# Moving low-part subtractions from GpSimd to VectorE, a scaling from VectorE to ScalarE, and repacing a weight conversion

## The chip, the cores and the metric

The kernel runs on one core of one Trainium2 chip. The metric is device time in microseconds (us) of one execution, and the median of several runs is quoted. The engines of a core each work through their own queue in program order: TensorE (PE in the rows; PEld is its weight load), VectorE (DVE), ScalarE (ACT), GpSimd (POOL) and SyncE (SP), which issues the DMAs.

## The reference

An attention layer over 2 batches, 8 heads, 576 positions and head width 64, with a position bias from a small network, gives 1152 rows of 512 values. Two gated layers follow, the second behind an RMS norm:

```python
def _moe_ref(x, w_gate, w_val, w_out):            # first layer
    gate = 1.0 / (1.0 + np.exp(-(x @ w_gate)))
    val = x @ w_val
    return (gate * val @ w_out).astype(np.float32)
...
    # second layer
    rms = np.sqrt(np.mean(x * x, axis=-1, keepdims=True) + 1e-06)
    xn = x / rms * rms_g
    g = xn @ w_gate
    silu = g * (1.0 / (1.0 + np.exp(-g)))
    val = xn @ w_val
    return (silu * val @ w_out).astype(np.float32)
```

`w_gate` and `w_val` are 512x1536, `w_out` is 1536x512. The weights arrive as 64-bit floating-point words.

## The kernel before, in words

Every product of the gated layers is made of three matmuls on rounded operands: a value is split in a high part (a copy to the type fp32r, on ScalarE) and a low part (the value less its high part). Names ending in `h` are high parts (`wh`, `xh`, `gh`, `nh`), names ending in `l` are low parts (`wl`, `xl`, `gl`, `nl`).

**Steps.** After the attention, the gated layers run as 72 steps `s`, a Python loop at L718 that writes out the order of all instructions by hand. A step is one block of 128 hidden columns (`f`) for one chunk of 384 rows (`c`). `STEPS` orders them by layer, group of blocks (`GROUPS`: 2, 3, 3, 4 blocks in the first layer, 4, 4, 4 in the second), chunk and block. In step `s` the program first calls `gate_val(s)`: 24 matmuls in two PSUM banks (L479), the gate on ScalarE (`sg`, L483), the product with it on VectorE (`g32`, shown as `g`, L485), its high part on ScalarE (`gh`, L487) and its low part (`gl`, L489). Then, between two halves of conversion work, it calls `out_mm(s - 2)`: 12 matmuls (L505) that add into two double banks `acc`. The PSUM pool `ps1` has four banks, so that `gate_val(s)` waits for the banks of step `s - 2`, which `sg` and `g` have to have read. A step whose successor has another group or chunk is called closing: after its `out_mm` the four banks are collected into `part` (L513, L515, L517), and the next `out_mm` can start only then. With blocks of 2, 3, 3, 4 and then 4 the closing `out_mm` falls in steps 3, 5, 7, 10, 13, and so on to 25, and then in every fourth step from 29 to 69.

**Norm.** When a chunk of the first layer is complete (in steps 29, 33 and 37), `norm_stage` runs in stages: squares on ScalarE and two adds on GpSimd (`nrm`, L544 to L546); two steps later a matmul that sums them (`ss`, L551) and a reciprocal root in small VectorE instructions (L555 to L567); one step later a matmul that spreads it (`rb` of L571), the scaling, and the split in `nh` (L577) and `nl` (L578). Step 36 is the first that reads `nh` and `nl`.

**Conversion.** The 72 weight pieces (128x512 each) are loaded as raw words (`wr`, three buffers) and converted. `piece_step(k, i)` has four parts, which this document calls by what they write: part 0 is `tt` (VectorE); part 1 is `ab` as an absolute value (ScalarE, L450), `ff` (VectorE, L452), `rb` (the low words scaled, L454) and the integer add of the two (GpSimd, L455); part 2 is the product `ab` (VectorE, L459) and `wh` (ScalarE, L460); part 3 is `wl` (VectorE, L464). `advance(limit, micro)` writes out up to `micro` parts that are ready, going round through the parts with the counter `phase`. In each half of a step the loop asks for 4 parts when the next piece is needed within 6 steps (`slack < 6`), else for 2. In the step where a closing `out_mm` falls the first half gets none. A piece is four parts.

Of the kernel before, what the change touches and what calls it, by code (L numbers as in the profile page):

```python
# [8 lines left out]
F32 = mybir.dt.float32  # L9
F32R = mybir.dt.float32r  # L10
U32 = mybir.dt.uint32
I32 = mybir.dt.int32
AF = mybir.ActivationFunctionType
ALU = mybir.AluOpType
# [7 lines left out]
NCC = DM // 128  # L22
NF = DFF // 128
CH = 384
# [44 lines left out]
def fused_kernel(ctx: ExitStack, tc: tile.TileContext, qk, vp, tab, pcol, invp, prm, wts, rg, out):  # L69
    nc = tc.nc  # L70
# [8 lines left out]
    def bank(nm):  # L79
        return ps1.tile([128, 512], F32, tag="one", name=nm)  # L80
# [335 lines left out]
    gt = {}  # L416
# [20 lines left out]
    def piece_step(k, i):  # L437
        mc = pools["mc"]
        if i == 0:
            tt = mc.tile([128, 512], U32, tag="tt", name=f"tt{k}")  # L440
            nc.vector.tensor_scalar(  # L441
                tt, wraw[k][:, :, 1], 3, 0x3FFFFFFF, op0=ALU.logical_shift_left, op1=ALU.bitwise_and
            )
            mid[k] = tt
        elif i == 1:
            raw = wraw.pop(k)
            lw, hw = raw[:, :, 0], raw[:, :, 1]
            tt = mid[k]
            ab = mc.tile([128, 512], F32, tag="ab", name=f"ab{k}", bufs=3)
            nc.scalar.activation(ab, hw.bitcast(F32), AF.Abs)  # L450
            ff = mc.tile([128, 512], U32, tag="ff", name=f"ff{k}", bufs=2)
            nc.vector.scalar_tensor_tensor(ff, hw, 0xC0000000, tt, op0=ALU.bitwise_and, op1=ALU.bitwise_or)  # L452
            rb = mc.tile([128, 512], I32, tag="rb", name=f"rb{k}")
            nc.vector.tensor_scalar(rb, lw, 2.0**-29, None, op0=ALU.mult)  # L454
            nc.gpsimd.tensor_tensor(ff.bitcast(I32), ff.bitcast(I32), rb, op=ALU.add)  # L455
            mid[k] = (ab, ff)
        elif i == 2:
            ab, ff = mid[k]
            nc.vector.scalar_tensor_tensor(ab, ab, TINY_HI, ff.bitcast(F32), op0=ALU.is_ge, op1=ALU.mult)  # L459
            nc.scalar.activation(ring[k % RING][0], ab, AF.Copy)  # L460
        else:
            ab, _ = mid.pop(k)
            hi, lo = ring[k % RING]
            nc.vector.tensor_tensor(lo, ab, hi.bitcast(F32), op=ALU.subtract)  # L464
            wp[PIECES[k]] = (hi, lo)

    def gate_val(s):
        l, g, c, f = STEPS[s]
        xhi, xlo = xs[l, c]
        mc = pools["mc"]  # L470
        pss = []
        for w in range(2):
            hi, lo = wp[l, f, w]
            ps = bank(f"gv{s}_{w}")
            k = 0
            for cc in range(NCC):
                cs = slice(cc * 128, cc * 128 + 128)
                for wt, xt in ((hi, xhi), (hi, xlo), (lo, xhi)):
                    nc.tensor.matmul(ps[:, :CH], wt[:, cs], xt[:, cc, :], start=(k == 0), stop=(k == 11))  # L479
                    k += 1  # L480
            pss.append(ps)
        sg = mc.tile([128, CH], F32, tag="sg", name=f"sg{s}")
        nc.scalar.activation(sg, pss[0][:, :CH], AF.Sigmoid if l == 0 else AF.Silu)  # L483
        g32 = mc.tile([128, CH], F32, tag="g32", name=f"g32_{s}", bufs=2)
        nc.vector.tensor_tensor(g32, pss[1][:, :CH], sg, op=ALU.mult)  # L485
        gh = mc.tile([128, CH], F32R, tag="gh", name=f"gh{s}", bufs=3)
        nc.scalar.activation(gh, g32, AF.Copy)  # L487
        gl = mc.tile([128, CH], F32R, tag="gl", name=f"gl{s}", bufs=3)
        nc.gpsimd.tensor_tensor(gl, g32, gh.bitcast(F32), op=ALU.subtract)  # L489
        gt[s] = (gh, gl)  # L490

    def out_mm(s):
# [44 lines left out]
    def norm_stage(c, stage, box):  # L537
        mc = pools["mc"]
        cs = slice(c * CH, c * CH + CH)
        sq = nrm[0][:, : NCC * CH].rearrange("p (a c) -> p a c", a=NCC)  # L540
        dg = nrm[0][:, NCC * CH : NCC * CH + 384].rearrange("p (a c) -> p a c", a=3)
        if stage == 0:
            for m in range(NCC):
                nc.scalar.activation(sq[:, m], part[m][:, cs], AF.Square)  # L544
            nc.gpsimd.tensor_tensor(sq[:, 0:2], sq[:, 0:2], sq[:, 2:4], op=ALU.add)
            nc.gpsimd.tensor_tensor(sq[:, 0], sq[:, 0], sq[:, 1], op=ALU.add)  # L546
            return
        if stage == 1:
            ssp = bank(f"ss{c}")
            for m in range(3):  # L550
                nc.tensor.matmul(  # L551
                    ssp[:, m : m + 1], sq[:, 0, m * 128 : m * 128 + 128], ones[:, 0:1], start=True, stop=True
                )
            ve = mc.tile([128, 3], F32, tag="ve", name=f"ve{c}")
            nc.vector.tensor_scalar(ve, ssp[:, 0:3], 1.0 / DM, 1e-6, op0=ALU.mult, op1=ALU.add)  # L555

            r0 = mc.tile([128, 3], F32, tag="r0", name=f"r0{c}")
            t1 = mc.tile([128, 3], F32, tag="t1", name=f"t1{c}")
            half = t1.bitcast(I32)
            nc.vector.tensor_scalar(half, ve.bitcast(I32), 1, None, op0=ALU.logical_shift_right)  # L560
            nc.vector.tensor_scalar(r0.bitcast(I32), half, -1.0, float(0x5F3759DF), op0=ALU.mult, op1=ALU.add)
            for _ in range(3):
                nc.vector.scalar_tensor_tensor(t1, r0, -0.5, r0, op0=ALU.mult, op1=ALU.mult)
                nc.vector.tensor_tensor(t1, t1, ve, op=ALU.mult)
                nc.vector.scalar_tensor_tensor(r0, t1, 1.5, r0, op0=ALU.add, op1=ALU.mult)
            for m in range(3):
                nc.vector.tensor_scalar(dg[:, m], ident, r0[:, m : m + 1], None, op0=ALU.mult)  # L567
            return
        rbp = bank(f"rb{c}")
        for m in range(3):  # L570
            nc.tensor.matmul(rbp[:, m * 128 : m * 128 + 128], ones, dg[:, m], start=True, stop=True)  # L571
        nh = xp.tile([128, NCC, CH], F32R, tag="xh", name=f"nh{c}")
        nl = xp.tile([128, NCC, CH], F32R, tag="xl", name=f"nl{c}")
        for m in range(NCC):
            x = part[m][:, cs]
            nc.vector.scalar_tensor_tensor(x, x, rgs[:, m : m + 1], rbp[:, :CH], op0=ALU.mult, op1=ALU.mult)
            nc.scalar.activation(nh[:, m], x, AF.Copy)  # L577
            nc.gpsimd.tensor_tensor(nl[:, m], x, nh[:, m].bitcast(F32), op=ALU.subtract)  # L578
        xs[1, c] = (nh, nl)

    done = [0, 0, 0, 0]
# [6 lines left out]
    def deadline(k):  # L588
        return USES[PIECES[k][:2]][0]

    def closing(s):
        return 0 <= s < NS - 1 and STEPS[s][:3] != STEPS[s + 1][:3]

    def ready(i):
        k = done[i]
# [12 lines left out]
    def advance(limit, micro):  # L608
        room[0] = limit
        idle = 0  # L610
        while micro and idle < 4:
            while loaded[0] < NPC and done[1] >= loaded[0] - 2:
                piece_load(loaded[0])
                loaded[0] += 1
            i = 3 - phase[0]
            phase[0] = (phase[0] + 1) % 4
            if ready(i):
                piece_step(done[i], i)
                done[i] += 1
                micro -= 1  # L620
                idle = 0
            else:
                idle += 1
# [94 lines left out]
    for s in range(NS + 2):  # L718
        while s < NS and (STEPS[s][0], STEPS[s][3], 1) not in wp:
            advance(done[3] + 1, 1)  # L720
        if 0 < s < NS:
            gate_val(s)
        for half in range(2):
            k = done[3]
            if k < NPC:
                lim = k
                while lim < NPC and lim < k + 3 and (lim < RING or released(lim - RING) <= s):
                    lim += 1
                slack = deadline(k) - s
                micro = 4 if slack < 6 else 2  # L730

                if closing(s - 2):
                    micro = (0, micro) [half] if slack > 1 else micro
                advance(lim, micro)
            if half == 0:
                if s > 1:
                    l, _, _, f = STEPS[s - 2]
                    while (l, f, 2) not in wp:
                        advance(done[3] + 1, 1)
                    out_mm(s - 2)  # L740
                while norm_queue and norm_queue[0][0] <= s:
                    _, c, stage, box = norm_queue.pop(0)
                    norm_stage(c, stage, box)
                    if stage < 2:
                        norm_queue.append([s + 2 - stage, c, stage + 1, box])


# [66 lines left out]
```

## Time and profile before

| what | value |
|---|---|
| median of 3 runs | 671.61 us (669.06 to 672.57) |
| the profiled execution's own time | 668.84 us |
| its span in the profile | 667.1 us |
| TensorE busy | 644.4 us, 97% of the span |
| VectorE busy | 494.6 us, 74% |
| ScalarE busy | 315.0 us, 47% |
| GpSimd busy | 316.6 us, 47% |

The span is what the profiler recorded between the first and the last instruction; 1.7 us of the execution's own time lie outside it. Busy shares are means over stages of very different kinds, and a matmul counts as busy until its modelled end, so consecutive matmuls overlap in the rows.

### The profile page before, as it was taken

To read this page: it belongs to the slowest core of one execution; us is meant where nothing else is said; L and a number is where in the kernel's file an instruction comes from. 1 tells how busy PE (TensorE), PEld (TensorE's weight loads), DVE (VectorE), ACT (ScalarE), POOL (GpSimd) and SP (SyncE) were. 2 spreads that over 40 slices of the span, in tenths; PEclk is the share of its full clock that TensorE was granted. 3 is DMA by queue.
4 is the path that set the end of the run, shared out by engine and by line. 5 is a ranking of instruction groups with operands and counts; after the bars stand their busy time and mean duration, and the time that the engine had idled before them with its cause. 6 is when DMAs were issued, how large, how long until landed. Compare 5 with 4: busy or idle time off the path is not lost.

```text
span 667.1 us, 11785 instructions
## 1 busy us (share of the span) xinstructions
PE 644.4 (97%) x4354; PEld 573.8 (86%) x4354; DVE 494.6 (74%) x965; ACT 315.0 (47%) x671; POOL 316.6 (47%) x319
## 2 busy tenths in 40 slices
PE   9799999999999799999999999889999999999997
PEld 5245557776689799999999999889999999999997
DVE  7699985788889986887799679989959658621211
ACT  6357778998784443333343345353544323311110
POOL 2246555887675443453444456565735434311111
PEclk9899999999999999999999999989999999999999
DMA  6879768998523342231233311322214322000111
GB/s 186 251 260 306 239 192 260 298 279 279 175 90 110 118 127 64 94 126 65 83 108 103 98 56 62 116 74 64 85 73 127 95 63 64 1 1 0 49 49 47
DMA packets 31642, 82.35 MB, mean 123 GB/s; under 512 B 3552, under 2 KB 5216, under 8 KB 31584
## 3 DMA queue, kind: packets, MB, share of 16 engines
q1 hardware_dynamic: 30720, 80.42, 38.3%
q10 hardware_dynamic: 864, 1.18, 0.5%
q8 instruction: 34, 0.56, 0.3%
q14 instruction: 24, 0.20, 0.1%
HBM read 68.33 MB, written 13.25 MB: 122 GB/s over the span
## 4 chain that ended last, share of the span: by engine, by line
PE 77%; DVE 12%; DMA 5%; issue 3%; ACT 1%; POOL 1%; SPq 1%; DVEq 0%; ACTq 0%; POOLq 0%
PE gv L479 40%; PE pv L369 4%; PE tp L349 4%; PE bps L190 4%; PE s L272 3%; DMA bias_d<-be 2%; DMA bt<-bias_d 2%; DVE ab L459 2%; DVE ff L452 2%; DVE t L290 1%; PE s L266 1%; DVE ht L176 1%; DVE tt L441 1%; DVE rb L454 1%; DVE wv L464 1%
## 5 line engine op out<-in xcount | busy, mean ns | idle before, releaser
L489 POOL TENSOR_TENSOR gl<-g,gh 128x384 fp32r<-128x384 f32 x72 | 85.9, 1192 | 165.0 <-ACT gh L487 165.0
L455 POOL TENSOR_TENSOR ff<-ff,rb 128x512 int32<-128x512 int32 x72 | 95.1, 1321 | 98.8 <-DVE rb L454 96.1
L485 DVE TENSOR_TENSOR g<-gv,sg 128x384 f32<-128x384 f32 x72 | 40.0, 555 | 114.1 <-PE gv L479 102.1
L487 ACT ACTIVATE gh<-g 128x384 fp32r<-128x384 f32 x72 | 37.9, 526 | 132.9 <-DVE g L485 131.5
L479 PE MATMUL gv<-xh,wh 128*128 128x384 f32 x240 | 81.1, 338 | 0.0
L479 PE MATMUL gv<-xh,wl 128*128 128x384 f32 x240 | 80.8, 336 | 0.0
L479 PE MATMUL gv<-xl,wh 128*128 128x384 f32 x240 | 80.7, 336 | 0.0
L460 ACT ACTIVATE wh<-ab 128x512 fp32r<-128x512 f32 x54 | 34.2, 633 | 76.2 <-DVE ab L459 75.7
L323 POOL TENSOR_SCALAR p<-p,rs 128x576 f32<-128x576 f32 x72 | 62.3, 876 | 15.9 <-DVE rs L321 13.0
L459 DVE SCALAR_TENSOR_TENSOR ab<-ab,ff 128x512 f32<-128x512 f32 x72 | 67.2, 933 | 1.2 <-POOL ff L455 1.2
L479 PE MATMUL gv<-nh,wh 128*128 128x384 f32 x192 | 65.4, 341 | 0.0
L479 PE MATMUL gv<-nl,wh 128*128 128x384 f32 x192 | 65.0, 338 | 0.0
L479 PE MATMUL gv<-nh,wl 128*128 128x384 f32 x192 | 64.9, 338 | 0.0
L483 ACT ACTIVATE sg<-gv 128x384 f32<-128x384 f32 x72 | 34.8, 484 | 59.2 <-PE gv L479 58.9
L290 DVE CUSTOM_DVE_ANT_0 t<-s,bt 128x576 f32<-128x576 f32 x72 | 51.7, 751 | 14.0 <-DMA bt<-bias_d 5.7
L176 DVE TENSOR_SCALAR ht<-w1l,bpc 128x448 f32<-128x448 f32 (+17 forms) x131 | 60.6, 527 | 2.1 <-PE bps L190 1.9
L464 DVE TENSOR_TENSOR wl<-ab,wh 128x512 fp32r<-128x512 f32 x54 | 62.1, 1149 | 0.0
L311 ACT ACTIVATE p<-t,mn 128x576 f32<-128x576 f32 x72 | 55.2, 768 | 8.8 <-DVE mn L290 8.6
L452 DVE SCALAR_TENSOR_TENSOR ff<-wr,tt 128x512 uint32<-128x512 uint32 x72 | 56.7, 787 | 0.0
L190 PE MATMUL bps<-ht,prms 128*32 128x264 f32 (+17 forms) x352 | 44.1, 493 | 5.5 <-DVE ht L176 4.4
L369 PEld LDWEIGHTS pv<-pt,v 128*64 128x64 f32 (+1 forms) x640 | 34.3, 136 | 16.3 <-ACT pt L656 4.0
L369 PE MATMUL pv<-pt,v 128*64 128x128 f32 (+3 forms) x640 | 48.1, 293 | 0.0
(455 smaller groups left out, 1588.1 us busy)
## 6 DMA issues: line engine op xcount, KB each, us to landing
wr<-wts SPq DMA_DIRECT2D x72, 512.0 KB, 3.6
bt<-bias_d SPq DMA_DIRECT2D x32, 576.0 KB, 5.1
bias_d<-be SPq DMA_DIRECT2D x36, 295.5 KB, 3.2
raw<-qk SPq DMA_DIRECT2D x16, 288.0 KB, 5.6
v<-vp SPq DMA_DIRECT2D x8, 480.0 KB, 6.3
bt<-bias_d SPq DMA_DIRECT2D x16, 144.0 KB, 5.2
out<-part SPq DMA_DIRECT2D x6, 192.0 KB, 1.9
out<-part ACTq DMA_DIRECT2D x6, 192.0 KB, 1.9
```

The lines of the kernel that those rows point to most:

```text
L176: nc.vector.tensor_scalar(ht, src, bpc[:, t : t + 1], 0.0, op0=ALU.add, op1=ALU.max)
L190: nc.tensor.matmul(ps[cg * 32 : cg * 32 + 32, :cut], prms[:, 2:34], hs[cg][:, a : a + cut], start=True, stop=True)
L290: nc.vector.tensor_tensor_reduce(t, sp[:, :, :288], bt[:, j].rearrange("p (a c) -> p a c", a=2), -SCALE, 3.0e38, ALU.add, ALU.min, mn[:, j ...
L311: nc.scalar.activation(p[:, j], t.rearrange("p a c -> p (a c)"), AF.Exp, bias=mn[:, j : j + 1], scale=-1.0, accum_out=sm[:, j : j + 1],)
L323: nc.gpsimd.tensor_scalar(p[:, j], p[:, j], rs[:, j : j + 1], 1.0, op0=ALU.mult, op1=ALU.mult)
L369: nc.tensor.matmul(box["ps"][j * 64 : j * 64 + 64, :n], v[:k, 2 * j if it == 4 else j, c, :], pt[:k, c, j * 64 : j * 64 + 64] if it == 4 e ...
L452: nc.vector.scalar_tensor_tensor(ff, hw, 0xC0000000, tt, op0=ALU.bitwise_and, op1=ALU.bitwise_or)
L455: nc.gpsimd.tensor_tensor(ff.bitcast(I32), ff.bitcast(I32), rb, op=ALU.add)
L459: nc.vector.scalar_tensor_tensor(ab, ab, TINY_HI, ff.bitcast(F32), op0=ALU.is_ge, op1=ALU.mult)
L464: nc.vector.tensor_tensor(lo, ab, hi.bitcast(F32), op=ALU.subtract)
L479: nc.tensor.matmul(ps[:, :CH], wt[:, cs], xt[:, cc, :], start=(k == 0), stop=(k == 11))
L489: nc.gpsimd.tensor_tensor(gl, g32, gh.bitcast(F32), op=ALU.subtract)
```

## The change

The low parts `gl` and `nl` and the two adds of the norm go from GpSimd to VectorE. The scaling `rb` goes from VectorE to ScalarE. `gl` is written out by a function of its own, after the first half of the step's conversion. The norm's adds get a stage of their own, one step after the squares, so that the two later stages fall in the same steps as before. The counter `phase` starts at another part. A new function `pace(s)` decides the number of parts of a whole step: 2 while a stage of the norm is due, 8 when the next piece is needed within 6 steps, else 4, split over the halves, or all of them in the second half where a closing `out_mm` falls.

```diff
-            nc.vector.tensor_scalar(rb, lw, 2.0**-29, None, op0=ALU.mult)
+            nc.scalar.activation(rb, lw, AF.Copy, scale=2.0**-29)
...
-        gl = mc.tile([128, CH], F32R, tag="gl", name=f"gl{s}", bufs=3)
-        nc.gpsimd.tensor_tensor(gl, g32, gh.bitcast(F32), op=ALU.subtract)
+        gt[s] = (gh, g32)
+
+    def low_part(s):
+        gh, g32 = gt[s]
+        gl = pools["mc"].tile([128, CH], F32R, tag="gl", name=f"gl{s}", bufs=3)
+        nc.vector.tensor_tensor(gl, g32, gh.bitcast(F32), op=ALU.subtract)
         gt[s] = (gh, gl)
...
-            nc.gpsimd.tensor_tensor(sq[:, 0:2], sq[:, 0:2], sq[:, 2:4], op=ALU.add)
-            nc.gpsimd.tensor_tensor(sq[:, 0], sq[:, 0], sq[:, 1], op=ALU.add)
             return
         if stage == 1:
+            nc.vector.tensor_tensor(sq[:, 0:2], sq[:, 0:2], sq[:, 2:4], op=ALU.add)
+            nc.vector.tensor_tensor(sq[:, 0], sq[:, 0], sq[:, 1], op=ALU.add)
+            return
+        if stage == 2:
...
-            nc.gpsimd.tensor_tensor(nl[:, m], x, nh[:, m].bitcast(F32), op=ALU.subtract)
+        for m in range(NCC):
+            x = part[m][:, cs]
+            nc.vector.tensor_tensor(nl[:, m], x, nh[:, m].bitcast(F32), op=ALU.subtract)
...
+    def pace(s):
+        if any(q[0] <= s for q in norm_queue):
+            return 2
+        return 8 if done[3] < NPC and deadline(done[3]) - s < 6 else 4
...
-            i = 3 - phase[0]
+            i = (2, 1, 0, 3)[phase[0]]
...
+        micro = pace(s)
+
+        parts = (0, micro) if closing(s - 2) else (micro // 2, micro - micro // 2)
         for half in range(2):
             k = done[3]
             if k < NPC:
...
-                slack = deadline(k) - s
-                micro = 4 if slack < 6 else 2
-
-                if closing(s - 2):
-                    micro = (0, micro) [half] if slack > 1 else micro
-                advance(lim, micro)
+                advance(lim, parts[half])
             if half == 0:
+                if s < NS:
+                    low_part(s)
                 if s > 1:
...
-                    if stage < 2:
-                        norm_queue.append([s + 2 - stage, c, stage + 1, box])
+                    if stage < 3:
+                        norm_queue.append([s + 1, c, stage + 1, box])
```

## Rows read from the trace of the kernel before

**Rows 1.** Busy time by stretch: start:end, length, each engine's busy us, clock, DMA.

```profile
120.00:190.00 70.00, 67.38 (x687) 50.28 (x684) 58.28 (x158) 60.65 (x158) 54.25 (x68) 1.00 0.78 241
190.00:245.00 55.00, 50.74 (x307) 48.03 (x306) 49.31 (x75) 27.59 (x54) 29.97 (x25) 1.00 0.36 114
392.00:440.00 48.00, 43.76 (x252) 43.44 (x251) 43.07 (x81) 19.69 (x36) 25.73 (x20) 0.96 0.25 84
440.00:653.00 213.00, 213.00 (x1229) 212.50 (x1228) 126.13 (x201) 69.22 (x132) 82.52 (x67) 1.00 0.18 56
```

**Rows 2.** Waits of TensorE from 125 us on: total us, times, longest.

```profile
PE rb L571 <- DVE nrm L567: 4.2, 1, 4.2
PE acc001a L505 <- ACT part L517: 3.4, 1, 3.4
PE s L266 <- DVE mn L290: 1.3, 5, 0.4
PE tp L349 <- DVE pt L654: 1.3, 3, 0.7
PE acc002a L505 <- ACT part L517: 0.9, 1, 0.9
```

**Rows 3.** Chain that ended last, 385 to 470 us: start, us, what.

```profile
405.17 0.67 PE rb L571 x6
...
431.48 1.67 DVE wv L464
...
435.76 1.65 PE rb L571 x6
437.41 4.98 PE gv L479 x24
...
444.46 4.18 PE gv L479 x24
```

**Rows 4.** Timeline of VectorE: start, us, engine, line, operation, idle before in brackets.

```profile
232.92 0.42 DVE L441 TENSOR_SCALAR tt<-wr 128x512 uint32<-128x512 uint32 x1
233.26 1.78 DVE L464 TENSOR_TENSOR wl<-ab,wh 128x512 fp32r<-128x512 f32 x1
234.96 0.68 DVE L459 SCALAR_TENSOR_TENSOR ab<-ab,ff 128x512 f32<-128x512 f32 x1
235.56 0.68 DVE L452 SCALAR_TENSOR_TENSOR ff<-wr,tt 128x512 uint32<-128x512 uint32 x1
236.16 0.41 DVE L454 TENSOR_SCALAR rb<-wr 128x512 int32<-128x512 uint32 x1
...
237.28 0.56 DVE L485 TENSOR_TENSOR g<-gv,sg 128x384 f32<-128x384 f32 x1 [0.70 <-ACT sg L483]
...
279.04 0.56 DVE L485 TENSOR_TENSOR g<-gv,sg 128x384 f32<-128x384 f32 x1 [0.70 <-ACT sg L483]
...
287.32 0.56 DVE L485 TENSOR_TENSOR g<-gv,sg 128x384 f32<-128x384 f32 x1 [0.71 <-ACT sg L483]
...
414.31 2.35 DVE L452 SCALAR_TENSOR_TENSOR ff<-wr,tt 128x512 uint32<-128x512 uint32 x1
```

**Rows 5.** Timeline of ScalarE in the same stretch as Rows 4.

```profile
235.67 0.63 ACT L460 ACTIVATE wh<-ab 128x512 fp32r<-128x512 f32 x1 [2.38 <-DVE ab L459]
236.21 0.66 ACT L450 ACTIVATE ab<-wr 128x512 f32<-128x512 f32 x1
236.77 0.48 ACT L483 ACTIVATE sg<-gv 128x384 f32<-128x384 f32 x1
237.93 0.53 ACT L487 ACTIVATE gh<-g 128x384 fp32r<-128x384 f32 x1 [0.68 <-DVE g L485]
```

**Rows 6.** Timeline of GpSimd, the same stretch, and the norm's first add.

```profile
233.14 1.34 POOL L455 TENSOR_TENSOR ff<-ff,rb 128x512 int32<-128x512 int32 x1 [1.63 <-DVE rb L454]
236.72 1.29 POOL L455 TENSOR_TENSOR ff<-ff,rb 128x512 int32<-128x512 int32 x1 [2.24 <-DVE rb L454]
238.53 1.00 POOL L489 TENSOR_TENSOR gl<-g,gh 128x384 fp32r<-128x384 f32 x1 [0.52 <-ACT gh L487]
...
414.26 1.85 POOL L545 TENSOR_TENSOR nrm<-nrm 128x768 f32<-128x768 f32 x1 [0.41 <-ACT nrm L544]
```

## The prediction

> **What bounds the kernel now.** I read the busy time by stretch first [rows 1]. TensorE is busy in 213.0 of 213 us after 440 us and has holes in three stretches: 2.6 us in the attention (120 to 190), 4.3 us at the start of the gated layers (190 to 245) and 4.2 us around the first layer's end (392 to 440). VectorE is no bound on average, but it is busy for 43.1 of 48 us in the last of them. Then the waits of TensorE say who ended each hole [rows 2]: 3.4 and 0.9 us before the first out_mm of the second and third chunk (acc001a, acc002a), which wait for the collects; 4.2 us before rb of L571, in the norm; and 2.6 us in eight short waits for VectorE in the attention. The chain shows that the hole of 4.2 us costs more than itself [rows 3]: after it the six matmuls of rb take 1.65 us, not 0.67, and the next gate_val 4.98, not 4.18. That is 1.8 us at the lower of the two granted clocks (1.2 of 2.4 GHz); over the stretch of 48 us it makes the mean 0.96 [rows 1]. So about 10 us can be won in all, and anything that makes VectorE or ScalarE late at a closing step can be lost.
>
> The timelines show why VectorE is late [rows 4, 6]. Its instructions with SBUF operands alone do not run beside GpSimd's: wl at 233.26 took 1.78 us, because the add of 233.14 ran until 234.48; the next ab took 0.68. ff at 414.31 took 2.35 us behind the norm's first add, which ended at 416.11.
>
> **The change part by part.** Start to start, [rows 4 to 6] give VectorE 0.34 us for tt and for rb, 0.60 for ff, ab and wl, 0.47 for g (237.28, 0.56 less the 0.08 by which neighbours overlap); ScalarE 0.54 for wh, 0.56 for ab's absolute value, 0.48 for sg; GpSimd 1.29 for the add and 1.00 to 1.34 for its neighbours.
>
> *gl on VectorE.* GpSimd loses 1.00 us a step and with it up to as much blocking of VectorE; VectorE gets 0.47 us, taken as g's, since both have 384 columns (ends: 0.47, and 1.78 when an add blocks it as it does wl). It waits for gh on ScalarE. In a closing step no conversion stands between g and gl, and the collects are queued behind gl: g 0.47, hop 0.1, gh 0.53, hop 0.1, gl 0.47, so the collects start 1.2 us later after g than before. TensorE's next out_mm waits for them. Where VectorE is on time this hides behind out_mm and the next gate_val (6.2 us); where it is late it is paid in full.
>
> *The norm.* Two adds by 3 chunks: 1.85 us on GpSimd becomes about 0.9 and 0.5 on VectorE. The four nl become 4 x 0.47 on VectorE, behind the scaling. The steps that read nl come four steps after it (steps 32, 36 and 40 for 36, 40 and 44), so nothing is paid there; without that cover it would be 1.9 us a chunk.
>
> *rb on ScalarE.* No row shows it. The nearest is ab's absolute value, which reads the same strided words into 512 columns: 0.56 start to start. I take 0.57; the ends are 0.48 (sg, 384 columns) and 0.66 (the absolute value's whole duration). VectorE gains 0.34 a piece. But the add now waits for a longer way: rb stands behind wh in ScalarE's queue, and wh waits for ab of the piece before. The loop from one ab to the next is ab 0.60 + hop 0.11 (234.96 to 235.67 less 0.60), wh 0.54, absolute value 0.56, rb 0.57 + hop 0.17 (from rb's end at 236.57 to the add at 236.72 it was 0.15), add 1.29 + a hop taken as 0.11: 3.95 us a piece. Two pieces make 7.9 us, against a step of TensorE of 6.25 us. Before, a step with two pieces took 8.28 us from g to g (279.04 to 287.32) [rows 4], so such a step stays longer than TensorE's. sg of the next step is queued behind rb too.
> The Trainium skill (ScalarE: Activation LUTs, Rules for kernel authors) says to put a plain multiplication on VectorE and not on ScalarE. The rows agree on one instruction: 0.41 us for rb on VectorE, 0.66 for the ScalarE one like it. By that page's price (186 ns + 0.833 ns a column, 93 ns overlapped; an estimate from it, 0.52 us) the sum would be about 1 us lower.
>
> *Order of parts.* 3, 2, 1, 0 and 2, 1, 0, 3 are the same ring, entered at another place, and at the start only part 0 is ready. The order does not change: 0 us. The loads are issued as before, one a piece.
>
> *Pace.* This I counted out from the code. Parts written in steps 0 to 5: before 4, 6, 8, 4, 8, 4; after 4, 8, 8, 8, 8, 4. In steps 30 to 36: before 4, 4, 4, 4, 8, 6, 4; after 2, 2, 2, 8, 2, 2, 2. In steps 44 to 48: before 4, 4, 8, 6, 4; after 8, 8, 8, 8, 4. In neither is a piece finished later than the step that uses it. So the norm is relieved, and the work is put into two rows of four steps with two pieces each.
>
> *The queues laid out.* I put the parts in the code's order on the queues of VectorE, ScalarE, GpSimd and TensorE, from step 1 on, each starting when its queue and inputs are free, and not VectorE beside GpSimd. For the kernel before this gives g in steps 1 to 31 within 0.4 us of the trace (279.2 and 287.6 for the two rows named) and holes of 3.5 and 1.5 us for the 3.4 and 0.9 of [rows 2]. After:
> Steps 1 to 5: g falls behind the end of its gate_val by 2.0, 5.7, 7.4, 10.7 and 9.0 us: 7.9 us a step, 9.5 in step 3 (g, gl and collects ahead of two pieces), against 6.25. The first collect leaves a hole of 3.2 us (3.4 before). The second, in step 5, comes 4.8 us late; less the 0.6 that the layout gave too much there, 4.2, which is 3.3 more than now.
> Steps 33 to 37: the two pieces of step 33 put g of step 34 6.2 us back, the sums come 1.1 us late for ss; the hole of 4.2 us and the 1.8 of slow clock are gone.
> Steps 44 to 49: here tt and wl stand ahead of ab and must let the add pass first, so a step of two pieces takes 8.8 us. Lags of g: 0.3, 2.3, 6.5 (the closing of step 45 among them), 9.0, 11.6. gate_val(s + 2) needs the bank that sg of s frees, 8.35 us after gate_val(s) ends (two out_mm of 2.1 and a gate_val of 4.18). So gate_val(49) waits 0.8, gate_val(50) 2.5, and in step 49 gl and the collects make out_mm(48) wait 3.1: 6.4 us where there is no wait now. From step 52 on all is on time, and the last steps have no conversion: no change at the end.
> The attention: eight pieces pass part 1 in it, so eight rb leave VectorE's queue and join ScalarE's, which has 9 of 70 us to spare [rows 1]. The bounds are -2.6 us (all eight short waits go) and +4.6 (each rb's 0.57 is met by TensorE). The list of waits names VectorE there and never ScalarE [rows 2], so I take -0.5.
>
> **Sum.** -6.0 (hole and clock) + 1.1 (ss) + 3.3 (step 5) - 0.2 (first collect) + 6.4 (steps 49 and 50) - 0.5 (attention) = +4.1: 672.9 us beside this execution's 668.84 (span 667.1 and 1.7 around it). The median shown is 2.8 us above this execution, so 675.7 us. With rb at 0.48 it is 1.8 less, at 0.66 1.8 more.
>
> **The rivals.**
> *A wash.* Holes overlap with those that the layout has too long, and the waits of steps 48 to 50 stay under 3 us. For it: the lag passes the 8.35 us of the banks only in steps 47 and 48, by 0.7 and 3.2 us. Against: the layout met 31 steps. -3 to +2.5 us: 668.6 to 674.1, about 671.6.
>
> *The two-piece steps hold.* The other side: if the loop is under 3.4 us, four steps of it lose less than 2.5 us to TensorE, no bank is late, and the collects of steps 5 and 49 hide. Then only the gain stays: -6.0, and -1 at step 5 and in the attention: 664.6. For it: gl no longer blocks VectorE, and the sum of VectorE's own parts of a piece is only 2.1 us. Against: the loop's 3.95 us is of waits, which no row shortens. The Trainium skill (GPSIMD Engine Reference, Engine selection) gives the rule that elementwise work belongs on VectorE, GpSimd being about 2 times slower; by it all that is moved off GpSimd is gain, and it would come out here. The rows agree for the instruction (1.00 against 0.47).
> *Worse.* rb takes 0.66, +1.8, and the clock falls after the hole of step 5, which at 4.2 to 4.8 us is no shorter than the one after which it fell [rows 2, 3], +1.8; with the waits of step 50 it may fall once more. Together +7.7 to +9.5: 679.3 to 681.1. Against the clock: after the 3.4 us of the first collect nothing of the kind is in the rows named.
>
> **How the numbers follow.** Forecast 0.42 (its own range 673.5 to 678.5), wash 0.30, hold 0.16, worse 0.12. Half a per cent, about what tells two kernels apart here, is 3.4 us: slower is above 675.0, faster below 668.3. The forecast's case is above 675.0 for 0.35 of its 0.42, worse wholly: slower 0.47. Faster is hold, 0.16. The rest, 0.37, is the same. The range of 666 to 683 leaves out 0.10 of hold and 0.03 of worse; it takes in the ends of rb and all but the far ends of the attention.
>
> **What would show it.** gl on VectorE at 0.5 to 0.6 us and rb on ScalarE near 0.65. The waits of TensorE list no wait of rb for nrm of 4 us, one of acc002a for the collects of 3 us or more near 240, and between 505 and 530 us waits of gv for sg and of acc110a for collects, 6 us together, where now there are none. GpSimd's adds take 1.3 us, with idle time ended by ScalarE before them. Wrong if g to g in steps 45 to 47 is under 7.5 us, if rb is far from 0.57, or if a hole stays in the norm.

## The result and the profile after

The changed kernel takes 674.41 us (median of 20 runs, 671.98 to 677.09), the kernel before 670.01 us beside it (20 runs, 668.79 to 673.58): a ratio of 1.0053, 95% interval 1.0038 to 1.0068. It is slower by half a per cent, within the range of 666 to 683 and 1.3 us below the predicted 675.7. The profiled execution took 673.01 us (span 671.2), 4.17 more than the profiled one of before; the sum had +4.1. The medians differ by 4.40 us: the predicted 675.7 stood on a median of 671.61 for the kernel before, 1.6 us above the one measured beside the change.

The busy time by stretch, as in [rows 1] (the same columns):

```profile
120.00:190.00 70.00, 67.12 (x675) 50.00 (x674) 58.66 (x151) 62.90 (x163) 54.49 (x67) 1.00 0.76 237
190.00:245.00 55.00, 50.06 (x286) 47.16 (x285) 40.36 (x70) 34.36 (x66) 20.55 (x18) 0.94 0.37 116
392.00:440.00 48.00, 47.41 (x282) 47.12 (x281) 37.59 (x89) 24.03 (x45) 7.75 (x6) 1.00 0.21 67
440.00:650.00 210.00, 205.51 (x1175) 204.57 (x1175) 110.24 (x212) 78.12 (x149) 29.69 (x23) 0.99 0.18 55
...
225.00:230.00 5.00, 4.99 (x16) 4.99 (x17) 3.41 (x7) 1.80 (x3) 1.27 (x1) 0.50 0.22 71
525.00:530.00 5.00, 2.45 (x9) 2.13 (x8) 3.35 (x7) 2.31 (x6) 1.26 (x1) 0.77 0.33 105
```

VectorE is relieved in the gated layers: 49.3 to 40.4 us at their start, 43.1 to 37.6 around the norm, 126.1 of 213 us to 110.2 of 210 after 440; in the attention it isn't (58.3 to 58.7). GpSimd falls to 7.75 around the norm. TensorE gains in one stretch only: around the norm its holes shrink from 4.2 to 0.6 us and its clock is whole again. After 440 us, where it had no hole, it now has 4.5 us of them. And the last two lines show what the totals hide: after 225 us TensorE runs for 5 us at the lower of its two granted clocks (0.50 is 1.2 of 2.4 GHz), and for part of the stretch after 525.

The waits of TensorE from 125 us on, as in [rows 2], say who ended each hole:

```profile
PE acc001a L509 <- ACT part L521: 3.1, 1, 3.1
PE acc110a L509 <- ACT part L521: 2.5, 1, 2.5
PE s L266 <- DVE mn L290: 2.2, 5, 1.2
PE gv L479 <- ACT sg L483: 1.9, 1, 1.9
PE acc002a L509 <- ACT part L521: 1.8, 1, 1.8
PE ss L557 <- DVE nrm L552: 0.6, 1, 0.6
```

The wait of 4.2 us before the norm's rb (the matmul that spreads the root; elsewhere in what follows rb is the scaling of the low words) is gone, a short one for the sums (ss) is in its place, acc002a waits twice as long, and a gate_val and an out_mm (acc110a) of steps 50 and 48 wait as they never did. The chain of what ended last (start, us, what) shows what is late, here in step 2:

```profile
212.28 0.70 DVE ab L459
...
213.01 0.64 ACT wh L460
213.65 0.57 ACT ab L450
214.21 0.58 ACT rb L454
...
214.86 1.30 POOL ff L455
...
216.18 0.70 DVE ab L459
```

This is the predicted loop of a piece: 3.90 us from one ab to the next, 4.01 to the one after (220.19), and no engine of it is full (VectorE, the fullest, is busy for 5.7 us of these 7.9). So a two-piece step takes 7.91 us from g to g in step 2 and 7.89 in step 3. The costliest groups (busy us, mean ns, idle before and its releasers) add the durations:

```profile
L455 POOL TENSOR_TENSOR ff<-ff,rb 128x512 int32<-128x512 int32 x72 | 93.3, 1296 | 295.8 <-ACT rb L454 249.9 <-DVE ff L452 40.8 <-ACT sg L483 3.7
L459 DVE SCALAR_TENSOR_TENSOR ab<-ab,ff 128x512 f32<-128x512 f32 x72 | 51.7, 717 | 21.7 <-POOL ff L455 21.7
L454 ACT ACTIVATE rb<-wr 128x512 int32<-128x512 uint32 x72 | 47.5, 660 | 0.0
L493 DVE TENSOR_TENSOR gl<-g,gh 128x384 fp32r<-128x384 f32 x72 | 40.4, 561 | 18.8 <-ACT gh L487 18.8
```

Last the timeline of TensorE at the two holes after which the clock fell (idle before in brackets):

```profile
221.58 0.34 PE L479 MATMUL gv<-xh,wl 128*128 128x384 f32 x1
225.01 0.69 PE L509 MATMUL acc001a<-gh,wh 128*128 128x384 f32 x1 [3.09 <-ACT part L521]
...
229.01 0.52 PE L479 MATMUL gv<-xh,wh 128*128 128x384 f32 x1
...
233.97 0.34 PE L509 MATMUL acc001a<-gh,wh 128*128 128x384 f32 x1
...
527.99 0.69 PE L509 MATMUL acc110a<-gh,wh 128*128 128x384 f32 x1 [2.55 <-ACT part L521]
...
531.60 0.34 PE L479 MATMUL gv<-nh,wh 128*128 128x384 f32 x1
```

A matmul takes 0.52 us there, not 0.34. The out_mm at 225.01 takes 4.00 us and the gate_val at 229.01 4.96, where the plain 2.1 and 4.17 stand elsewhere: 2.7 us. The out_mm at 527.99 takes 3.61: 1.5 us.

### The profile page after: what moved, and what is told of

Read it like the earlier page. It is cut to its first block, busy times and chain, and to the rows that moved or that the text cites. A ratio compares the mean times of both kernels' runs of the same rounds, so it can differ in the third digit from the quotient of the medians.

```text
span 671.2 us, 11699 instructions
## 1 busy us (share of the span) xinstructions
PE 647.9 (97%) x4354; PEld 576.5 (86%) x4354; DVE 446.5 (67%) x983; ACT 354.3 (53%) x743; POOL 205.0 (31%) x229
## 4 chain that ended last, share of the span: by engine, by line
PE 72%; DVE 9%; ACT 8%; DMA 4%; POOL 4%; issue 2%; SPq 0%; DVEq 0%; ACTq 0%; POOLq 0%
PE gv L479 36%; PE bps L190 5%; PE pv L369 4%; PE s L272 4%; PE tp L349 4%; POOL ff L455 3%; DVE ab L459 3%; DMA bt<-bias_d 3%; ACT ab L450 2%; ACT rb L454 2%; ACT wh L460 2%; DVE t L290 1%; DVE ht L176 1%; PE s L266 1%; DMA wr<-wts 1%
## 5 line engine op out<-in xcount | busy, mean ns | idle before, releaser
L455 POOL TENSOR_TENSOR ff<-ff,rb 128x512 int32<-128x512 int32 x72 | 93.3, 1296 | 295.8 <-ACT rb L454 249.9
L323 POOL TENSOR_SCALAR p<-p,rs 128x576 f32<-128x576 f32 x72 | 62.0, 872 | 14.3 <-DVE rs L321 10.9
L459 DVE SCALAR_TENSOR_TENSOR ab<-ab,ff 128x512 f32<-128x512 f32 x72 | 51.7, 717 | 21.7 <-POOL ff L455 21.7
L493 DVE TENSOR_TENSOR gl<-g,gh 128x384 fp32r<-128x384 f32 x72 | 40.4, 561 | 18.8 <-ACT gh L487 18.8
L452 DVE SCALAR_TENSOR_TENSOR ff<-wr,tt 128x512 uint32<-128x512 uint32 x72 | 50.9, 707 | 0.0
L454 ACT ACTIVATE rb<-wr 128x512 int32<-128x512 uint32 x72 | 47.5, 660 | 0.0
```

What stands on the lines that cost most here:

```text
L323: nc.gpsimd.tensor_scalar(p[:, j], p[:, j], rs[:, j : j + 1], 1.0, op0=ALU.mult, op1=ALU.mult)
L454: nc.scalar.activation(rb, lw, AF.Copy, scale=2.0**-29)
```

## The experiments

Theory: what sets the time is where conversion is written out, not which engine does it. Two pieces in a step are longer than TensorE's step of 6.25 us, on the old engines and on the new ones; that costs in steps 1 to 5 and 44 to 50 what the calmer norm gains. Rival A: the moves gain and only the new pace costs, so the moves with the old pace win. Rival B: the moves cost (longer loop, gl ahead of the collects) and the pace is innocent. All kernels were timed beside the kernel before, whose median was 670.3 to 670.8 us in the three sets. With "hole" a wait of TensorE is meant.

**The moves with the old pace.**

```diff
-        micro = pace(s)
-        parts = (0, micro) if closing(s - 2) else (micro // 2, micro - micro // 2)
...
-                advance(lim, parts[half])
+                slack = deadline(k) - s
+                micro = 4 if slack < 6 else 2
+                if closing(s - 2):
+                    micro = (0, micro)[half] if slack > 1 else micro
+                advance(lim, micro)
```

> The change with the pace of before (per half 4 parts when the next piece is needed within 6 steps, else 2); all moves between engines stay. Theory (two pieces in one step are too long for either set of engines, and the pace decides where they stand): steps 44 to 50 have no hole, but the pieces stand beside the norm again, where VectorE now also has the norm's adds and low parts, so holes of 3 to 5 us come back at the norm (steps 35 to 38); by the queues laid out 668.3 where the kernel before has 660.0 and the change 666.4, so 674 to 678 us. Rival 1 (the moves gain, only the pace costs): faster than the kernel before, 664 to 668 us. Rival 2 (the moves cost, the pace is innocent): about the change's 674 us, with its holes in steps 49 and 50 still there.

Measured: 679.48 us (4 runs), ratio 1.0131 (1.011 to 1.0152). Waits of TensorE from 125 us on:

```profile
PE acc001a L509 <- ACT part L521: 3.7, 1, 3.7
PE acc100a L509 <- ACT nrm L548: 3.3, 1, 3.3
PE rb L577 <- DVE nrm L573: 2.2, 1, 2.2
...
PE acc012a L509 <- DVE part L517: 1.7, 1, 1.7
PE gv L479 <- ACT sg L483: 1.5, 1, 1.5
```

Rival A falls: the moves with the old pace lose 9 us. But only a part of that is lost around the norm, where the theory put it. In the profiled execution (11.4 us longer than that of before) TensorE comes 3.8 us later to the first out_mm, since its clock was low in the attention:

```profile
140.00:150.00 10.00, 9.59 (x56) 6.07 (x57) 7.72 (x20) 7.34 (x17) 7.49 (x7) 0.66 0.82 210
```

3.6 us more are lost up to acc012a, and 4.0 around the norm. There the old pace writes two pieces into step 34, gl, the adds and nl now stand on VectorE beside them, and three holes are where there was one; which of these makes them isn't shown, as they were moved together, and the adds also come a step later.

**The new pace with the old engines.** gl, nl and the adds go back to GpSimd, rb to VectorE; pace, stages and order of parts stay.

```diff
-            nc.scalar.activation(rb, lw, AF.Copy, scale=2.0**-29)
+            nc.vector.tensor_scalar(rb, lw, 2.0**-29, None, op0=ALU.mult)
...
+        gl = mc.tile([128, CH], F32R, tag="gl", name=f"gl{s}", bufs=3)
+        nc.gpsimd.tensor_tensor(gl, g32, gh.bitcast(F32), op=ALU.subtract)
```

> The kernel before with the change's pace alone (gl, nl and the norm's adds on GpSimd, rb on VectorE). Theory: the lengths of two-piece steps are much the same on the old engines (8.28 us), so the holes of step 5 (about 5 us) and of steps 49 and 50 (1 to 4 us) come as in the change and the hole of 4.2 us in the norm goes: 672 to 675 us. Rival 1 (the moves gain, the pace costs): slower than the change, 677 us or more. Rival 2 (the moves cost, the pace is innocent): at most 670 us, faster than the change by 4 us or more.

Measured: 672.77 us (11 runs), ratio 1.0043 (1.0027 to 1.006). Waits:

```profile
PE acc001a L511 <- ACT part L523: 4.8, 1, 4.8
PE acc002a L511 <- ACT part L523: 3.3, 1, 3.3
PE acc110a L511 <- ACT part L523: 2.2, 1, 2.2
```

Rival B falls: without any move the pace loses in the same three places, and gains in the norm (no hole there). Its steps 45 to 48 take 8.1 to 9.0 us, on other instructions: here wl takes 1.2 us in the mean (0.68 and 1.78 by turns), longer beside GpSimd's work. The loop through rb on ScalarE is one of two ways to be too long.

**rb alone back on VectorE.**

```diff
-            nc.scalar.activation(rb, lw, AF.Copy, scale=2.0**-29)
+            nc.vector.tensor_scalar(rb, lw, 2.0**-29, None, op0=ALU.mult)
```

> The change with the scaling rb back on VectorE. Theory: the loop from one ab to the next loses the way through ScalarE, and sg no longer stands behind rb: g to g in steps 46 and 47 falls from 8.5 to about 8.0 us, the wait of gate_val in step 50 from 1.9 to under 0.5; but the first collect comes later (VectorE has 0.34 more a piece), so 2 us less in sum, 672 to 673 us. Rival (rb is not what counts): the same as the change, 674 us, waits of steps 49 and 50 unchanged.

Measured: 673.6 us (9 runs), ratio 1.0042 (1.0021 to 1.0063), not to be told from the change's. The parts moved, though: steps 47 and 48 take 7.9 us instead of 8.5, no gate_val waits for sg, and the first two collects leave 4.4 and 2.5 us instead of 3.1 and 1.8. It is an exchange; the test doesn't separate the theories in total.

**gl behind the collects in closing steps.**

```diff
-                if s < NS:
+                if s < NS and not closing(s - 2):
                     low_part(s)
...
                     out_mm(s - 2)
+                if s < NS and closing(s - 2):
+                    low_part(s)
```

> The change with gl written behind out_mm and the collects in the steps where a closing out_mm falls, not ahead of them. Theory: the collects start about 1 us earlier after g, so the holes of steps 5 and 49 are 0.5 to 1 us shorter and the one before ss goes: 671 to 673 us. Rival (the collects wait for something else, or gl then comes late for its own out_mm): no difference, or holes before the out_mm two steps later.

Measured: 673.04 us (12 runs), ratio 1.0037 (1.0021 to 1.0054). Steps 4 and 46 become 0.7 us shorter (9.36 to 8.64 and 10.25 to 9.56), and the collects' holes nearly stay (3.1, 1.9, 2.2). gl's place is worth about a microsecond at most (the interval overlaps that of the change): too little to be the cause.

**One and a half pieces a step.** If the pace is what loses, fewer parts a step must win, on either set of engines: 6 parts are 5.9 us of the loop against 6.25.

```diff
-        return 8 if done[3] < NPC and deadline(done[3]) - s < 6 else 4
+        return 6 if done[3] < NPC and deadline(done[3]) - s < 5 else 4
```

> The changed kernel with one and a half weight pieces a step at most, not two (6 parts, not 8), when the next piece is needed within 5 steps (not 6). My theory (two pieces a step are longer than TensorE's step, on the loop from one ab to the next of 3.9 us a piece; 1.5 pieces are 5.9 us against 6.25): laid out with the durations of the rows, the holes of steps 5, 49 and 50 go, one of 1.7 us at a collect of step 25 is new, 14 us less than the laid-out changed kernel less what that layout has too much there: 661 to 665 us, faster than before by 5 to 9 us. Rival (VectorE and ScalarE have too much work in the stretches of the closings whatever the pace, so that less now is missing later): 672 to 676 us, the holes moved to later steps.

Measured: 660.12 us (5 runs), ratio 0.9856 (0.9833 to 0.988). Where the change had five holes from 190 us on, one is left:

```profile
PE s L266 <- DVE mn L290: 2.0, 4, 1.3
PE acc030a L509 <- DVE part L517: 1.2, 1, 1.2
```

It is 14.3 us below the change, and the holes did not move to later steps: the rival falls. By VectorE's timeline steps 1 to 5 now have 4, 4, 6, 6 and 6 parts, and steps 44 to 48 have 4, 6, 6, 6 and 6. The edit lowers two numbers at once. For the late steps a run further down has 6 parts with the 6 steps kept; for the early ones no run tells the two apart. The same pace with gl behind the collects:

> The kernel with 6 parts a step at most, and gl written after the collects in the closing steps. Theory: the collects start 1.2 us sooner after g, so that the hole of step 25 goes too: 659 to 664 us, 0 to 2 us less than with 6 parts alone. Rival (gl then comes late for the out_mm two steps later): a new wait of out_mm for gl, and no gain.

Measured: 659.35 us (5 runs), ratio 0.9848 (0.9822 to 0.9873); the hole of acc030a falls to 0.4 us. And the same pace with the old engines (the edit of the second experiment and this one):

> The kernel before (gl, nl and the norm's adds on GpSimd, rb on VectorE) with the change's pace, at 6 parts a step at most and within 5 steps. Theory (the pace is what loses and what gains, and the moves matter little once no step is longer than TensorE's): 662 to 666 us, 6 us or more below before, within 2 us of the changed kernel at this pace. Rival (the moves are needed, since VectorE blocked by GpSimd takes up to 1.8 us for wl): over 668 us, with holes at the collects that the changed kernel at this pace does not have.

Measured: 659.47 us (4 runs), ratio 0.9839 (0.982 to 0.9858). Two views of it, the waits and the groups of VectorE:

```profile
PE s L266 <- DVE mn L290: 1.5, 6, 0.4
...
PE acc010a L511 <- ACT part L523: 0.6, 1, 0.6
PE gv L479 <- DVE wv L464: 0.2, 1, 0.2
```
```profile
L464 DVE TENSOR_TENSOR wl<-ab,wh 128x512 fp32r<-128x512 f32 x54 | 71.7, 1328 | 0.0
L459 DVE SCALAR_TENSOR_TENSOR ab<-ab,ff 128x512 f32<-128x512 f32 x72 | 67.3, 935 | 1.9 <-POOL ff L455 1.9
```

This decides it. wl takes 1.33 us in the mean here and 0.69 in the changed kernel, where gl is off GpSimd, and TensorE waits for no wl, only once for 0.2 us for a value weight's low part (wv, the same line). With work spread evenly the moves that the change is made of are worth nothing that these runs can tell.

> The kernel with 6 parts a step at most and gl after the collects, with rb on VectorE again. Theory: with the loop of a piece shorter than TensorE's step whatever rb's engine, rb's place is worth less than 1 us: 659 to 664 us, the same as with rb on ScalarE. Rival (rb on ScalarE pays, since it takes 0.34 us a piece off VectorE, which the collects and g stand on): 1 us or more slower, with a hole before an out_mm of a new chunk; or (rb on ScalarE costs in the chain) 1 us or more faster.

Measured: 658.59 us (5 runs), ratio 0.9839 (0.9811 to 0.9867), the lowest median, with no hole after 190 us. The four intervals overlap: rb's engine is worth under a microsecond at this pace, as expected, though the time lies 0.4 us below the range named.

**Which of the two rushes costs what.** The pace of 8 parts up to step 19 and 6 from there on, and the other way round:

```diff
-        return 8 if done[3] < NPC and deadline(done[3]) - s < 6 else 4
+        most = 8 if s < 20 else 6
+        return most if done[3] < NPC and deadline(done[3]) - s < 6 else 4
```

> The changed kernel with 8 parts a step up to step 19 and 6 from step 20 on. Theory: the first two collects keep their holes (3.1 and 1.8 us, and slow TensorE after the first), and the losses of steps 49 and 50 go, predicted at 6.4 us, with them the sums' wait of the norm, predicted at 1.1 us: 7.5 us below the change, 665 to 669 us. Rival (VectorE and ScalarE have too much work after the norm at any pace): 672 us or more.

Measured: 668.57 us (12 runs), ratio 0.997 (0.9952 to 0.9988). Only the two early collects are left of the gated layers' holes:

```profile
PE acc002a L509 <- ACT part L521: 2.9, 1, 2.9
PE acc001a L509 <- ACT part L521: 2.9, 1, 2.9
```

```diff
-        return 8 if done[3] < NPC and deadline(done[3]) - s < 6 else 4
+        most, near = (6, 5) if s < 20 else (8, 6)
+        return most if done[3] < NPC and deadline(done[3]) - s < near else 4
```

> The changed kernel with 6 parts a step up to step 19 (when the next piece is needed within 5 steps), 8 from step 20 on (within 6). Theory: the two holes of the first collects go, predicted at 3.2 and 4.2 us, and one of up to 2 us at the collect of step 25 is new; the losses of steps 49 and 50 stay: 5 to 7 us below the change, 667 to 670 us. Rival (a slower start makes pieces late, and the holes move to steps 7 to 13): 672 us or more.

Measured: 666.32 us (7 runs), ratio 0.9932 (0.9908 to 0.9956). The late ones are left, and acc030a's:

```profile
PE acc110a L509 <- ACT part L521: 2.5, 1, 2.5
...
PE gv L479 <- ACT sg L483: 1.9, 1, 1.9
PE acc030a L509 <- DVE part L517: 1.5, 1, 1.5
PE ss L557 <- DVE nrm L552: 0.6, 1, 0.6
```

Against 674.41 the late rush costs 5.8 us and the early one 8.1; together 13.9, where both cured at once gave 14.3. They add up, as far as medians with intervals of 0.3 to 0.5% tell.

**The rule of 2 parts beside the norm, taken out.**

```diff
     def pace(s):
-        if any(q[0] <= s for q in norm_queue):
-            return 2
```

> The changed kernel without the rule of 2 parts a step beside the norm; 8 or 4 parts as for every other step. Theory (the norm's rule puts the conversion off, so that it is owed in steps 44 to 48, four steps with two pieces each): with 8 parts before the norm pieces are ready enough that 4 parts a step do beside it, no hole in the norm and none in steps 49 and 50: 7.5 us below the change, 665 to 669 us. Rival (the rule is what took away the norm's wait, as the prediction says, worth 6 us): 676 to 680 us.

Measured: 669.17 us (12 runs), ratio 0.9971 (0.9946 to 0.9996).

```profile
PE acc001a L509 <- ACT part L521: 3.1, 1, 3.1
PE s L266 <- DVE mn L290: 1.8, 4, 1.0
PE acc002a L509 <- ACT part L521: 1.7, 1, 1.7
PE acc100a L509 <- ACT nrm L548: 0.2, 1, 0.2
```

The norm's hole stays away without its rule, and the losses of steps 48 to 50 go with it: 5.2 us faster than the change. In the profiled executions it is 7.1 us from the first out_mm on, near the 7.5 expected; the attention before it was 3.8 us slower, with a clock of 0.66 from 140 to 150 us. Counted out from the code: with 8 parts 42 pieces are ready after step 28 (40 in the kernel before), and steps 30 to 36 then get 4, 4, 4, 4, 6, 4, 4 parts, steps 44 to 48 four each. With the rule it is 2, 2, 2, 8, 2, 2, 2, and the debt is paid as 8, 8, 8, 8, 4 in steps 44 to 48. The same edit at 6 parts:

> The changed kernel at 6 parts a step at most (within 5 steps) and without the rule of 2 parts beside the norm. Theory: at 6 parts the conversion isn't ahead when the norm comes, so that beside it there are steps of 6 parts, and holes of 1.8 to 3.7 us at the norm's collects and its spreading matmul come back: 5 to 8 us above the kernel with 6 parts and the rule, 665 to 668 us. Rival (VectorE, freed of rb, has room for both): 658 to 661 us.

Measured: 665.24 us (6 runs), ratio 0.9912 (0.9887 to 0.9937), 5.1 us above 6 parts with the rule:

```profile
PE acc032a L509 <- ACT nrm L548: 1.8, 1, 1.8
PE acc100a L509 <- ACT nrm L548: 1.3, 1, 1.3
PE acc030a L509 <- DVE part L517: 1.2, 1, 1.2
```

So the rule has no price of its own. It pays where the pace behind it keeps the debt under TensorE's step, and costs where the debt comes back as two-piece steps.

Eight of the twelve medians lie outside the range named before the run: four above it by up to 1.5 us (the moves with the old pace), four below it by up to 2.5 us (the old engines at 6 parts). The laid-out queues gave the order of the kernels, and their distances less well. Two pieces of the change were in every run and never tested alone: the order of parts and the norm's adds as a stage of their own.

## Why the prediction came out right

The start of the same step's g on VectorE's timelines (us from the span's start), after less before, shows where the time came and went:

| step | before | after | difference |
|---|---|---|---|
| 1 | 208.20 | 207.28 | -0.92 |
| 8 | 252.18 | 255.40 | +3.22 |
| 31 | 396.25 | 399.34 | +3.09 |
| 43 | 481.79 | 479.29 | -2.50 |
| 60 | 588.27 | 592.45 | +4.18 |
| 71 | 657.09 | 661.24 | +4.15 |

*Attention: -0.5 predicted, -0.3 measured* (the last matmul ahead of acc001a's hole starts 0.3 us sooner, 221.58 against 221.89). That it holds is luck of this execution: among the nine profiles with rb on ScalarE it is the only one whose first out_mm is earlier than in the kernel before, and the others are 0.3 to 3.9 us later. The last section shows what differs there.

*Steps 2 to 8: +3.1 predicted, +3.5 measured* (-0.3 to +3.22). The mechanism was right, the size of its parts wrong. The first collect left 3.1 us (3.2 predicted, 3.4 before). The second left 1.85, not 4.2: TensorE came to it 2.7 us late, by the slow clock. By rows, 3.1 - 3.4 + 2.6 (out_mm 4.00 against 2.19 at the same place before, gate_val 4.96 against 4.16) + 1.85 - 0.9 makes 3.25. The step that failed is "after the 3.4 us of the first collect nothing of the kind": after 3.1 us the clock fell. It hardly changed the sum, which is luck too, since the chain from 212 us to acc002a at 242.26 runs over VectorE, ScalarE and GpSimd alone: slow matmuls filled the hole. So of the signs named, a hole of 3 us or more before acc002a did not come.

*Norm: -6.0 and +1.1, -4.9 predicted, -5.6 measured* (+3.09 to -2.50). The hole before the spreading matmul and the slow clock behind it went, ss waited 0.6 and not 1.1. But "so the norm is relieved" was put down to the 2 parts beside it, and that is wrong: without them g of step 43 is 5.9 us nearer than g of step 31 (+6.81 to +0.87 against before). With two more pieces ready, and the moves in place, no hole over 0.2 us is left there.

*Steps 44 to 50: +6.4 predicted, +6.7 measured* (-2.50 to +4.18). Steps 45 to 48 take 8.18, 10.25, 8.52 and 8.49 us, where the predicted lags make 8.25, 10.45, 8.75 and 8.85. The small excess of the layout adds up: gate_val(49) didn't wait (0.8 predicted), gate_val(50) waited 1.94 (2.5), out_mm(48) 2.55 (3.1). That is 4.5 us of holes, not 6.4. 1.5 us of slow clock behind them, of which the sum had none, make it 6.0, and the rest lies in the starts and ends of the matmuls around the holes. That the term came out so near is chance.

*rb.* In the chain it takes 0.55 to 0.60 us, about the value taken, with 0.66 for the whole instruction. That 0.09 us more would be 1.8 us of time is not shown: rb back on VectorE made the late steps 0.2 to 0.7 us shorter each and the time no different, as VectorE then came later to the first collects. "The two-piece steps hold" fell: the loop was 3.9 us, not under 3.4. The Trainium skill (GPSIMD Engine Reference, Engine selection) puts elementwise work on VectorE and not on GpSimd. The trace agrees for one instruction (gl 0.56 us on VectorE, 1.00 on GpSimd [rows 6]). But 5 to 9 us less VectorE time in a stretch moved the end only where VectorE ended a wait.

*What the prediction did not say.* Both terms that lose are one cause, two pieces in one step, and the pace alone brings it. That two-piece steps already took 8.28 us before stood among its rows; that such steps are best never written was not drawn from it, and it was worth 11 us to either set of engines.

## What to carry to other kernels

Before moving work between engines, lay out how much of it falls into one step of the bound engine and compare the longest chain of that step with the step's length; spreading the same work evenly, with the 2 parts beside the norm, gave 1.5% here on the old engines and on the new, and the moves gave nothing on top. A rule that puts work off beside a critical place must be read with the place where the work comes back. An engine's busy share, or an instruction's price on another engine, says little where no wait of the bound engine ends on it.

## What was not expected of the hardware

TensorE's granted clock fell to 0.50 after a hole of 3.1 us at 221.9 us in the changed kernel, and stayed whole after one of 3.4 us at 222.2 us in the kernel before. In both TensorE was busy for 31.0 of 31 us from 190 to 221. The stretch from 225 us on in the kernel before, whose hole ends at 225.63:

```profile
225.00:230.00 5.00, 4.37 (x25) 4.37 (x26) 4.30 (x9) 2.49 (x6) 2.19 (x2) 1.00 0.29 79
```

That profile of the kernel before is the exception. Seven other profiles have a hole of 2.9 to 4.8 us at this place (the changed kernel and six of the runs above), and in all seven the clock of the five us from the hole's end on is 0.50 or 0.66. Nor is the execution a common one: its mean clock is 0.995, and of 58 other executions of the kernel before that were timed beside the runs, 51 have 0.984 to 0.991. Where those lost it isn't recorded, but the prediction's argument that the clock stays whole here rested on one execution. What decides it stays open; the price is to be read from rows at the lower clock: 2.7 us here, 1.5 us after the hole of 2.5 us at 525.

In the attention the fall differs between profiles of kernels whose attention is written out alike. The stretch of 140 to 150 us, first in the changed kernel, then in the kernel with 6 parts a step:

```profile
140.00:150.00 10.00, 9.65 (x98) 6.78 (x96) 9.27 (x24) 9.94 (x27) 9.25 (x10) 1.00 0.85 211
```
```profile
140.00:150.00 10.00, 9.53 (x55) 6.09 (x56) 7.96 (x22) 7.36 (x17) 7.50 (x7) 0.66 0.77 224
```

g of step 0 starts at 193.86 us in the first and at 198.06 in the second. With rb on ScalarE each of nine profiles has a wait of s for mn of 0.7 to 1.5 us near 140, and in five of them the clock of this stretch is 0.66 or 0.83. With rb on VectorE the longest such wait is 0.4 us in all five profiles, and the clock is 1.00. So rb's move, whose longest wait there is only some 0.8 us longer, may cost 3 to 4 us in an execution in which the clock falls. Fourteen profiles suggest it; no run was made to show it, and the times at 6 parts (658.59 and 659.35 us) don't tell the two apart. One of the five executions with rb on VectorE there (662.02 us, mean clock 0.991, the others 0.994 to 0.996) lost clock somewhere too.
